# A feed-forward first product by Strassen's scheme over pairs of chunks, in a transformer kernel whose second stage is ordered by timed lines

## The chip, the cores and the metric

The kernel runs on one core of one Trainium2 chip. The metric is the device time of one execution in microseconds; a trace of one profiled execution is there beside it. TensorE (PE in the profile) multiplies matrices, with PEld as its weight load; VectorE is DVE, ScalarE is ACT, GpSimd is POOL, and SyncE (SP) issues nearly all transfers.

## What is computed

Two layers, each an attention block without a softmax over keys and a feed-forward block, on x of 2048 rows (tokens) and 640 columns, all float32:

```python
x = x + A(layernorm(x), wqkv, wo)
x = x + B(layernorm(x), w1, b1, w2, b2)      # and both once more

def A(x, wqkv, wo):                          # 32 heads of 20
    q, k, v = split(x @ wqkv)
    pq, pk = phi(q), phi(k)                  # phi(t) = (t > 0 ? t + 1 : exp(t)) + 1e-6
    kv, z = sum_s(pk[s] v[s]^T), sum_s(pk[s])
    return (pq @ kv / (pq @ z + 1e-6)) @ wo
def B(x, w1, b1, w2, b2):                    # 640 -> 1728 -> 640
    r = max(x @ w1 + b1, 0)
    return (r * r) @ w2 + b2
```

Each float32 operand of a matmul is split into a high and a low part (`split`: ACT copies the value rounded to PE's float32r, DVE subtracts it from the value), and a product is three matmuls: high x low, low x high, high x high (`mm3`, L404 to L408).

## The kernel before, in words

**Tiles and stages.** The 2048 tokens are 16 tiles of 128; four tiles are a group, so there are NG = 4 groups. The 1728 hidden columns are NF = 14 chunks of 128, the last of 64. 640 columns are DC = 5 blocks of 128. In each layer a first stage goes over the 16 tiles (layer norm, q, k and the sums over tokens) and a second stage does the feed-forward over the four groups.

**First stage.** `part` (L494) makes q and k of a tile, `g_part` and `gt_part` the sums over tokens. In layer 0 the `Prep` class (L264) also loads the feed-forward weights, splits them and stores the halves to memory as 24 "units" of 640 KB, two or three a tile by `PREP`. `k_post` (L686) adds k's rows on POOL (L693).

**Second stage, per group and chunk.** `fc1` (L1238) computes a chunk of hidden values for 512 tokens: 5 blocks x 3 matmuls = 15, 512 columns each, in one go into one bank of PSUM; chunk 13 has both halves in one weight tile and takes 10. `act` (L1271) reads the bank: ACT adds b1 and takes the relu (L1276) and the square (L1277), DVE squares again in full (L1280) and makes the low half (L1281); the four instructions follow one another. `fc2` (L1378) multiplies the chunk of the step before with w2: four tiles of 3 matmuls of 512 columns, and a strip of 3 for the last 128 columns of the output, all accumulating in five banks over the 14 chunks. So PE's order is fc1(c), fc2(c-1), fc1(c+1) and so on, each with its long run.

**Side work.** While a group is in the feed-forward, the attention output of the next group's tiles is made beside it: `side` (L1626) puts each step of it at a place (chunk, position after the i-th tile of fc2) from the tables `fast`, `OUTS`, `OUT0` (L38 to L81). Per two tiles it is seven block products of 320 columns (`Pair`, L1500), Strassen's scheme on the product with the 640 x 640 matrix M, whose results go to two banks in turn (`po0`, `po1`); then layer norm, a transpose in blocks of 32 (`blocks_T`, and `blocks_move`, L386, 16 small copies by ACT), the split (`x_split`, L1490) and the addition of b2 to the residual on DVE (`f_bias`, L672, L675). These tables were written by hand; no planner is in the kernel.

**Weights.** Chunks 4 and 7 stay in SBUF (`RESIDENT`); the other units go through a ring of six tiles (`Units`, L298): a used tile is loaded again by `load_ring` (L309, issue L315) from the SP queue. `x1_load`, `x2_store` and the tile loads use the same queue.

**End of a group.** With the last chunk the four accumulated tiles are added to the residual by DVE (`tile_add`, L1372); the strip goes through DVE's transpose and 16 small copies (L1337, L1347, L1365).

Of the kernel before, what the change touches and what calls it, by code (L numbers as in the profile page):

```python
# [13 lines left out]
P = 128  # L14
# [5 lines left out]
NF = 14  # L20
# [8 lines left out]

HR = 6 * DH  # L30
# [5 lines left out]
RESIDENT = (4, 7)  # L36
RING = 6
LATE = ((9, 11, 12, 13, 14, 15), (8, 9, 11, 13, 14, 15))  # L38

PREP = {t: 2 if t > 5 else 3 for t in range(2, 12)}  # L40
# [6 lines left out]
def pair_plan(m0, m1, turn, out, back):  # L47

    return {"blocks0": m0, "blocks1": m1, "turn": turn, "out": out, "back": back}


def fast(b):
    return pair_plan(
        b - 3, b - 2, [(b - 1, 0), (b - 1, 1), (b - 1, 2), (b - 1, 3)],
        {"p1": (b, 0), "p4": (b, 1), "p6": (b, 2), "p7": (b, 3), "p5": (b, 4),
         "p2": (b + 1, 0), "p3": (b + 1, 2)},
        [((b, "post"), (b + 1, 0), (b + 1, 1), (b + 2, 0), (b + 2, 1), (b + 3, 0)),
         ((b + 1, 3), (b + 1, "post"), (b + 2, 0), (b + 2, "post"), (b + 3, "pre"), (b + 3, 4))],
    )

STRIP = ((6, 0), (6, 2), (6, 4), (7, 0), (7, 2))

OUT0 = (fast(4), fast(9))
STAY = 1
FB0 = 0
# [8 lines left out]
LOW_AT = 1  # L76
OUTS = (
    {**fast(2), ("den", 0): ((-4, "post"), (-3, 1)), ("den", 1): ((-3, "post"), (-2, 1)),
     "split1": ((0, "pe"), (0, "post"))},
    fast(9),  # L80
)  # L81

# [6 lines left out]
def kernel(  # L89
# [30 lines left out]
    FB = {"h": 0, "po1": 1, "as": 2, "a0": 3, "a1": 4, "a2": 5, "a3": 6, "po0": 7}  # L120
# [35 lines left out]
    def src_plain(w, r0, c0):  # L156
        return lambda v: [(v, w[r0 : r0 + P, c0 : c0 + D])]

# [9 lines left out]
    def src_w2(c):  # L168
        if c < 13:
            return src_plain(w2, c * P, 0)  # L170
        return lambda v: [(v[:FL], w2[13 * P :, :]), (v[FL:], w2[13 * P :, :])]
# [62 lines left out]
    for g in range(NG):  # L234
        for c in range(NF):
            uses.append((g, "w1", c))
            if c > 0 or g > 0:
                uses.append((g if c else g - 1, "w2", (c - 1) % NF))
    uses.append((NG - 1, "w2", NF - 1))

    def src_unit(nm, c):
        return src_w1(c) if nm == "w1" else src_w2(c)

    def unit_len(nm, c):
        return DC * P if (nm, c) == ("w1", 13) else 2 * D

    def unit_parts(nm, c, u, raw):
        if (nm, c) == ("w1", 13):
            w = u.rearrange("p (d f) -> p d f", d=DC)
            return w[:, :, :FL], w[:, :, FL:], raw[:, : DC * FL].rearrange("p (d f) -> p d f", d=DC)  # L250
        return u[:, :D], u[:, D:], raw

    def split_high(*unit):
        hi, lo, raw = unit_parts(*unit)
        nc.scalar.activation(hi, raw, AF.Copy)

    def split_low(*unit):
        hi, lo, raw = unit_parts(*unit)
        nc.vector.tensor_tensor(out=lo, in0=raw, in1=hi.bitcast(F32), op=ALU.subtract)
# [4 lines left out]
    class Prep:  # L264


        def __init__(self):
            self.todo = [(nm, c) for g, nm, c in uses if g == 0 and c not in RESIDENT]
            self.raws, self.halves, self.done = [], [], []

        def load(self):
            if self.todo:
                nm, c = self.todo.pop(0)
                raw = ftile("st")
                for d, s in src_unit(nm, c)(raw):
                    nc.sync.dma_start(d, s)
                self.raws.append((nm, c, raw))

        def high(self):
            if self.raws:  # L280
                nm, c, raw = self.raws.pop(0)
                u = utile("uprep")[:, : unit_len(nm, c)]
# [3 lines left out]
        def low(self):  # L286
            if self.halves:
                nm, c, u, raw = self.halves.pop(0)
                split_low(nm, c, u, raw)
                self.done.append((nm, c, u))  # L290
# [7 lines left out]
    class Units:  # L298


        def __init__(self):
            self.at = {}
            self.pairs = {}
            self.ring = [u for u in uses if u[2] not in RESIDENT]
            self.stay = [u for u in uses if u[0] == 0 and u[2] in RESIDENT]
            self.free = 0
            self.raws, self.halves = [], []

        def load_ring(self):  # L309

            while self.ring and self.free > 0:
                self.free -= 1
                g, nm, c = self.ring.pop(0)
                u = utile("u")[:, : unit_len(nm, c)]
                nc.sync.dma_start(u.bitcast(F32), kept[nm, c])  # L315
                self.at[g, nm, c] = u

        def place(self):
            _, nm, c = self.stay.pop(0)
            if nm == "w1":  # L320
                self.pairs[c] = wtile("uw")
            i = 2 * D * (nm == "w2")
            self.at[0, nm, c] = u = self.pairs[c][:, i : i + 2 * D]
            return nm, c, u

        def raw_stay(self, dst):

            if len(self.raws) < len(self.stay):
                _, nm, c = self.stay[len(self.raws)]
                for d, s in src_unit(nm, c)(dst):  # L330
                    nc.sync.dma_start(d, s)
                self.raws.append(dst)

        def split_stay(self):
            if self.raws:
# [1428 lines left out]
```

## Time and profile before

| | |
|---|---|
| median of 3 runs | 1334.89 us (1334.78 to 1335.19) |
| span of the profiled execution | 1333.5 us, first to last instruction |
| granted PE clock | 1.000 over the whole span |
| PE / PEld / DVE / ACT / POOL busy | 1328.7 / 1153.0 / 902.6 / 709.0 / 122.8 us |
| second stage, layer 0 and layer 1 | about 249 to 670 us, and 909 us to the end |
| memory traffic | 257.74 MB, 193 GB/s over the span |

The profiled execution's own time is its span and about 1.4 us around it, if it is like the median run. In a row of groups stand the line, engine and operation, the tiles written and read, the shapes and the count; then busy time and the mean of one in ns; then the engine's idle time ahead of them. A matmul's own duration (389 ns for 512 columns) is from its start to its modelled end; matmuls overlap, so their pace is read from start to start. In the table of stretches each engine has its busy time and its count, then come the granted clock, the share of the DMA engines and GB/s.

### The profile page before, as it was taken

To read this page: it belongs to the slowest core of one execution; us is meant where nothing else is said; L and a number is where in the kernel's file an instruction comes from. 1 tells how busy PE (TensorE), PEld (TensorE's weight loads), DVE (VectorE), ACT (ScalarE), POOL (GpSimd) and SP (SyncE) were. 2 spreads that over 40 slices of the span, in tenths; PEclk is the share of its full clock that TensorE was granted. 3 is DMA by queue.
4 is the path that set the end of the run, shared out by engine and by line. 5 is a ranking of instruction groups with operands and counts; after the bars stand their busy time and mean duration, and the time that the engine had idled before them with its cause. 6 is when DMAs were issued, how large, how long until landed. Compare 5 with 4: busy or idle time off the path is not lost.

```text
span 1333.5 us, 18816 instructions
## 1 busy us (share of the span) xinstructions
PE 1328.7 (100%) x6751; PEld 1153.0 (86%) x6751; DVE 902.6 (68%) x1629; ACT 709.0 (53%) x1638; POOL 122.8 (9%) x172
## 2 busy tenths in 40 slices
PE   9999999999999999999999999999999999999998
PEld 8888999988888888888888899998888888888887
DVE  8988888877856766543367678788767567665323
ACT  5888855644544436524547686564534435454131
POOL 1222220000000000000012232100000000000000
PEclk9999999999999999999999999999999999999999
DMA  6788837575656566488521115176547565564654
GB/s 207 260 303 319 273 97 235 195 257 181 220 186 216 153 242 200 150 315 295 194 99 51 49 40 148 40 258 257 177 148 280 149 204 201 194 225 142 245 168 158
DMA packets 101075, 257.74 MB, mean 193 GB/s; under 512 B 12854, under 2 KB 38070, under 8 KB 100310
## 3 DMA queue, kind: packets, MB, share of 16 engines
q1 hardware_dynamic: 99470, 253.85, 56.1%
q10 hardware_dynamic: 1512, 2.69, 0.7%
q8 instruction: 53, 0.87, 0.3%
q14 instruction: 40, 0.33, 0.1%
HBM read 197.80 MB, written 60.13 MB: 193 GB/s over the span
## 4 chain that ended last, share of the span: by engine, by line
PE 100%; ACT 0%; POOL 0%; issue 0%; DVE 0%; POOLq 0%
PE PS L408 38%; PE PS L1321 28%; PE PS L1258 28%; PE PS L429 3%; PE PS L1011 1%; PE PS L1040 1%; PE PS L756 1%; PE PS L557 0%; PE PS L377 0%; PE PS L956 0%; PE PS L773 0%; PE PS L1361 0%; ACT kq L201 0%; ACT xT L777 0%; DVE x L1372 0%
## 5 line engine op out<-in xcount | busy, mean ns | idle before, releaser
L1258 PE MATMUL PS<-xTb,u 128*128 128x512 f32 x1400 | 332.8, 389 | 0.0
L396 ACT ACTIVATE z<-y 32x160 f32<-32x160 f32 x880 | 294.0, 334 | 60.2 <-DVE y L383 50.3
L1258 PEld LDWEIGHTS PS<-xTb,u 128*128 128x128 f32 x1400 | 262.2, 188 | 53.9
L408 PE MATMUL PS<-kq,xT 128*128 128x320 f32 (+2 forms) x1575 | 282.0, 333 | 0.0
L1321 PE MATMUL PS<-u,h 128*128 128x512 f32 (+1 forms) x1125 | 279.7, 389 | 0.0
L408 PEld LDWEIGHTS PS<-kq,xT 128*128 128x128 f32 x1575 | 250.3, 188 | 24.9
L1276 ACT ACTIVATE hr<-PS,b1sb 128x512 f32<-128x512 f32 x104 | 71.5, 687 | 349.2 <-PE PS L1258 347.8
L1321 PEld LDWEIGHTS PS<-u,h 128*128 128x128 f32 x1125 | 208.4, 188 | 39.5
L1280 DVE TENSOR_TENSOR hr<-hr 128x512 f32<-128x512 f32 x104 | 71.3, 685 | 149.5 <-ACT h L1277 149.4
L408 PE MATMUL PS<-kh,xh 128*128 128x512 f32 x480 | 124.3, 392 | 0.0
L367 POOL TENSOR_SCALAR rs<-mv 128x1 f32<-128x1 f32 x62 | 27.9, 450 | 854.7 <-DVE mv L365 854.7
L408 PEld LDWEIGHTS PS<-kh,xh 128*128 128x128 f32 x480 | 87.1, 188 | 14.6
L511 ACT ACTIVATE e<-PS 128x320 f32<-128x320 f32 (+4 forms) x128 | 53.2, 435 | 85.0 <-PE PS L408 77.8
L518 DVE TENSOR_SCALAR e<-e 128x320 f32<-128x320 f32 (+4 forms) x128 | 41.1, 321 | 57.6 <-ACT e L511 57.4
L1321 PE MATMUL PS<-h,u 128*128 128x512 f32 x280 | 79.1, 390 | 0.0
L1281 DVE TENSOR_TENSOR h<-hr,h 128x512 fp32r<-128x512 f32 x104 | 72.0, 693 | 7.8 <-DVE hr L1280 0.5
L693 POOL TENSOR_TENSOR acc<-acc,r 128x640 f32<-128x640 f32 x28 | 50.7, 1811 | 190.0 <-DVE r L519 190.0
L1277 ACT ACTIVATE h<-hr 128x512 fp32r<-128x512 f32 x104 | 65.8, 633 | 3.3
L1321 PEld LDWEIGHTS PS<-h,u 128*128 128x128 f32 x280 | 52.0, 188 | 10.5 <-DVE h L1294 0.4
L1536 DVE TENSOR_TENSOR xr<-PS,xr 128x320 f32<-128x320 f32 x48 | 23.5, 489 | 51.5 <-PE PS L408 50.2
L1258 PE MATMUL PS<-xTb,uw 128*128 128x512 f32 x240 | 57.0, 389 | 0.0
L519 DVE SCALAR_TENSOR_TENSOR r<-PS,e 128x512 f32<-128x512 f32 (+2 forms) x104 | 51.1, 492 | 5.8 <-ACT e L511 2.2
(146 smaller groups left out, 1576.4 us busy)
## 6 DMA issues: line engine op xcount, KB each, us to landing
u<-kept_w SPq DMA_DIRECT2D x184, 640.0 KB, 4.7
x<-x SPq DMA_DIRECT2D x48, 320.0 KB, 5.2
kept_w<-uprep SPq DMA_DIRECT2D x23, 640.0 KB, 5.4
pqt<-pq SPq DMA_DIRECT2D x128, 80.0 KB, 4.5
x<-xr SPq DMA_DIRECT2D x32, 320.0 KB, 2.2
st<-in_B_w_dram SPq DMA_DIRECT2D x22, 320.0 KB, 4.1
pq<-r SPq DMA_DIRECT2D x20, 320.0 KB, 2.3
kept_kq<-kq SPq DMA_DIRECT2D x10, 640.0 KB, 6.8
```

The source lines that it names most:

```text
L396: nc.scalar.activation(d, v, AF.Copy)
L408: nc.tensor.matmul(ps, a, b, start=first and i == 0, stop=last and i == 2)
L511: nc.scalar.activation(self.e[:, a:b], ps, AF.Exp)
L518: nc.vector.tensor_scalar(e, e, 1.0, PHI_EPS, op0=ALU.min, op1=ALU.add)
L519: nc.vector.scalar_tensor_tensor(out=self.r[:, a:b], in0=ps, scalar=0.0, in1=e, op0=ALU.max, op1=ALU.add)
L693: nc.gpsimd.tensor_tensor(out=acc, in0=acc, in1=r, op=ALU.add)
L1258: nc.tensor.matmul(ps, a[:, d, :], bb[:, d, :], start=n == 0, stop=n == len(order) - 1)
L1276: nc.scalar.activation(r, ps, AF.Relu, bias=b1sb[:, c : c + 1])
L1277: nc.scalar.activation(h[:, 0], r, AF.Square)
L1280: nc.vector.tensor_tensor(out=r, in0=r, in1=r, op=ALU.mult)
L1281: nc.vector.tensor_tensor(out=h[:, 1], in0=r, in1=h[:, 0].bitcast(F32), op=ALU.subtract)
L1321: nc.tensor.matmul(ps, l, r, start=(first or new) and k == 0, stop=end and k == len(a) - 1)
```

## The change

**The product.** Chunks 0 to 11 of `fc1` are taken in six pairs. For a pair, the four inner blocks of 640 (two and two, `E`, `F`, `G`, `H` are the weights' combinations) and two halves of 256 tokens make a 2 x 2 product of blocks, done with seven block products where eight were; the fifth block of 128 is done as before (`rest`, 512 columns). The class `Strassen` has five segments: `seg1` (two products, 12 matmuls of 256 columns), `seg2` (one, 6), `seg3` (three, 18), `seg4` (one, 6, and 3 of 512 columns), `seg5` (3 of 512). Partial results are shared by copies between PSUM banks: `copy1` (two by ACT), `copy2` (one by ACT), `add1` and `add2` (DVE). Two banks are used, `h` and `h1`; `h1` takes the place of `po1`, so that the side products have one bank. Tiles stand in the order `POS = (0, 2, 1, 3)` in the group.

```diff
+            def seg1(self):
+                self.product(self.h1[:, :HG], self.w("E", 0), self.x(0, 0), True)
+                self.product(self.h1[:, HG:], self.w("H", 0), self.t("u", 0))
+            def copy1(self):
+                self.s7 = hr_tile("s7")[:, :HG]
+                nc.scalar.activation(self.h0[:, :HG], self.h1[:, :HG], AF.Copy)
+                nc.scalar.activation(self.s7, self.h1[:, HG:], AF.Copy)
+            def seg2(self):
+                self.product(self.h1[:, :HG], self.w("G", 0), self.t("u", 1))
+            def copy2(self):
+                nc.scalar.activation(self.h0[:, HG:], self.h1[:, :HG], AF.Copy)
+            def add1(self):
+                l = self.h1[:, :HG]
+                nc.vector.tensor_tensor(out=l, in0=l, in1=self.s7, op=ALU.add)
+            def seg3(self):
+                self.product(self.h0[:, :HG], self.w("E", 1), self.x(1, 0))
+                self.product(self.h0[:, HG:], self.w("H", 1), self.t("v", 0))
+                self.product(self.h1[:, :HG], self.w("F", 0), self.t("v", 1))
+            def add2(self):
+                nc.vector.tensor_tensor(out=self.h1[:, HG:], in0=self.h0[:, HG:], in1=self.s7, op=ALU.add)
+            def seg4(self):
+                self.product(self.h0[:, HG:], self.w("G", 1), self.x(1, 1))
+                self.rest(self.h0, 1)
+            def seg5(self):
+                self.rest(self.h1, 0)
```

**What it needs beside it.** The weights' combinations are made in the first stage of layer 0 by four sums per pair on POOL, and stored as units of 512 KB; `w2` of chunks 8 to 11 is split only in the second stage. The tokens' combinations are four sums per two tiles, on DVE or POOL (`t_sums`), and splits of them (`t_split`). The addition of b2 goes from DVE to POOL.

```diff
+        def sums(self, c):
+            r0, r1 = self.pair[c]
+            ...
+                nc.gpsimd.tensor_tensor(out=out, in0=x, in1=y, op=op)
...
+        def t_sums(t, eng):
+            ...
+                eng[0].tensor_tensor(out=out, in0=x, in1=y, op=ALU.subtract)
...
         def f_bias(t):
             v = xr.pop(t)
-            nc.vector.tensor_tensor(out=v, in0=v, in1=b2bc, op=ALU.add)
+            nc.gpsimd.tensor_tensor(out=v, in0=v, in1=b2bc, op=ALU.add)
+            yield
             nc.sync.dma_start(x1d[t], v)
...
-RESIDENT = (4, 7)
 RING = 6
+STEPS = (("p", 13), ("p", 12), *(("w", i) for i in range(NW)))
+FIRST, LAST = 13, 11
+POS = (0, 2, 1, 3)
...
-PREP = {t: 2 if t > 5 else 3 for t in range(2, 12)}
+AFTER = 8
+PREP = {t: 4 if t in (3, 5, 7) else 3 for t in range(2, 13)}
```

No chunk is resident any more; the ring has seven tiles, and a group reads 40 units in the order of their use.

**The order.** The hand-written tables go. A planner, the class `Clock`, keeps a time for each engine and for the transfers, with costs in the code (for instance 0.14 us and 0.95 ns a column on ACT, 0.08 us and 1.04 ns on DVE, 0.2 us and 2.4 ns on POOL, n x (columns/2400 + 0.0133) us on PE). The work is a list of "lines", generators that yield an engine, a cost and the function that issues the instructions, or a need (`need`, `until`, a free buffer). `run` always issues PE's next step from the line that can go on first (by rank where equal), after `fill` has issued all work of the other engines that ends by then. So the order is fixed when the program is built. `fc1_line` is:

```diff
+                    yield "PE", pe_cost(12, HG), st.seg1
+                    yield "until", lambda: slots["hr"]
+                    yield "ready", ck.chain(
+                        "ACT", 2 * cost("ACT", HG), st.copy1, max(main.ready, free[0], take("hr"))
+                    )
+                    yield "PE", pe_cost(6, HG), st.seg2
+                    at = main.ready
+                    yield "ready", ck.chain("ACT", cost("ACT", HG), st.copy2, at)
+                    yield "ready", ck.chain("DVE", cost("DVE", HG), st.add1, at)
+                    yield "PE", pe_cost(18, HG), st.seg3
+                    yield "ready", ck.chain("DVE", cost("DVE", HG), st.add2, main.ready)
+                    yield "PE", pe_cost(6, HG) + pe_cost(3, GT), st.seg4
+                    turned(g, 2 * c, st.h0, 0)
+                    yield "PE", pe_cost(3, GT), st.seg5
+                    turned(g, 2 * c + 1, st.h1, 1)
```

`fc2_line` yields one step per tile (3 matmuls), `pair_line` one per block product, and `x_line`, `t_line`, `q_line`, `strip_line`, `ring_line`, `next_line` the rest; a block move can go to ACT or DVE, a square or a sum to DVE or POOL, whichever the planner has free first.

1052 lines of the change are left out of this document (713 added, 339 removed).

## The prediction

> **What bounds the kernel now.** I read the first page, then PE's waits, the chain of work, the groups by form, and a few stretches in order of time.
>
> ```profile
> span 1333.5 us, 18816 instructions
> PE 1328.7 (100%) x6751; PEld 1153.0 (86%) x6751; DVE 902.6 (68%) x1629; ACT 709.0 (53%) x1638; POOL 122.8 (9%) x172
> PE 100%; ACT 0%; POOL 0%; issue 0%; DVE 0%; POOLq 0%
> ```
> ```profile
> PE PS L557 <- POOL ident masks.py:199: 1.4, 1, 1.4
> ```
>
> TensorE is busy from end to end, the chain that ends last is PE alone, and in PE's list of waits there is one entry, 1.4 us before the first transpose. So every matmul taken away shows in full, and every wait that is added shows in full too. A "busy PE" could still hide slow matmuls, so their real pace comes next, from starts:
>
> ```profile
> 699.73 0.85 PE L408 MATMUL PS<-kh,xh 128*128 128x512 f32 x3
> 700.42 1.95 PE L408 MATMUL PS<-kq,xT 128*128 128x256 f32 x15
> 702.21 0.86 PE L408 MATMUL PS<-kh,xh 128*128 128x512 f32 x3
> ```
> ```profile
> 1320.51 5.67 PE PS L1321 x25
> ```
> ```profile
> L1258 PE MATMUL PS<-xTb,u 128*128 128x512 f32 x1400 | 332.8, 389 | 0.0
> L408 PE MATMUL PS<-kq,xT 128*128 128x256 f32 x285 | 37.1, 282 | 0.0
> L1258 PE MATMUL PS<-xTb,uw 128*128 128x512 f32 x240 | 57.0, 389 | 0.0
> ```
>
> Twenty-five matmuls of 512 columns took 5.67 us: 0.2268 each. Fifteen of 256 columns took 702.21 - 700.42 = 1.79 us from first start to next start: 0.119 each, each with weights of its own. I use 0.120. The busy time of that group gives 37.1/285 = 0.130; it counts the last one's tail beside the next matmul, so it is the upper bound.
>
> **The change, part by part.**
>
> *Products.* The first product now has 1400 + 240 = 1640 matmuls of 512 columns (205 in each of 8 groups of tokens). Behind the change a group has six pairs of chunks, each with 42 matmuls of 256 and 6 of 512, beside chunks 12 and 13 as before (25 of 512): 252 and 61, so 2016 and 488 in all. Gone: 1152 x 0.2268 = 261.3. New: 2016 x 0.120 = 241.9. Net **-19.4 us**; with 0.119 it is -21.4, with 0.130 +0.8. The second product and the seven-product pairs of the attention output keep their matmuls.
>
> [...] The sum goes by the rows.
>
> *New waits.* Before, a chunk was one unbroken run of 15 matmuls into one bank. Now a pair is five segments (12, 6, 18, 9 and 3 matmuls), and between them ACT copies quarters of PSUM (three copies of 256 columns) and DVE adds (two). PE's next segment waits for these; what is queued behind the waiting matmul on PE is everything else, so it must be covered by matmuls put between. Prices:
>
> ```profile
> 600.14 3.56 PE L1258 MATMUL PS<-xTb,uw 128*128 128x512 f32 x15
> 603.54 2.88 PE L1321 MATMUL PS<-u,h 128*128 128x512 f32 x12
> 603.74 0.69 ACT L1276 ACTIVATE hr<-PS,b1sb 128x512 f32<-128x512 f32 x1 [5.45 <-PE PS L1258]
> ```
> ```profile
> L511 ACT ACTIVATE e<-PS 128x256 f32<-128x256 f32 x19 | 7.3, 385 | 0.4
> L1468 DVE TENSOR_TENSOR z<-z 128x256 f32<-128x256 f32 x48 | 20.4, 424 | 1.5
> L1372 DVE TENSOR_TENSOR x<-PS,x 128x512 f32<-128x512 f32 x32 | 20.9, 685 | 27.8 <-PE PS L1321 20.0 <-DMA x<-x 7.8
> L1498 DVE TENSOR_TENSOR xTb<-z,xTb 128x640 fp32r<-128x640 f32 x24 | 19.7, 822 | 29.5 <-ACT xTb L1496 29.5
> L675 DVE TENSOR_TENSOR xr<-xr,b2bc 128x640 f32<-128x640 f32 x32 | 26.0, 814 | 0.0
> L693 POOL TENSOR_TENSOR acc<-acc,r 128x640 f32<-128x640 f32 x28 | 50.7, 1811 | 190.0 <-DVE r L519 190.0
> ```
>
> From the next matmul's start to ACT's start: 603.74 - 603.54 = 0.20 us. With an estimate of 0.05 back to PE, two copies cost 0.20 + 2 x 0.385 + 0.05 = 1.02, one copy 0.64, one addition 0.67. In the order in which the changed program issues PE's instructions, most gaps hold six matmuls of the second product (1.36 us), so they are covered with 0.34 and 0.7 to spare. Uncovered are: the first pair of each layer, where nothing stands in the first two gaps (1.02 + 0.64, twice: **3.3 us**); and the step from the first group to the second in layer 0, where DVE is to split the last tile of the second group only behind the four additions of the first group's output, and PE has nothing left (0.20 + 0.685 + 0.82 + 0.05 = **1.75 us**). Lower bound for the other gaps is nothing; the upper bound stands with the rivals.
>
> *VectorE and ScalarE.* Both have room: DVE is busy 68%. Per layer the change adds 48 additions, 32 or so sums and 16 splits to DVE and takes 16 biases off it (0.814 each); ACT gets 72 copies and 16 splits and loses about a tenth of its block moves. Taken off an engine that PE does not wait for, this gains nothing.
>
> *POOL.* The 32 additions of b2 go to POOL, as do 24 sums of weights in the first stage and some 28 short sums beside the feed-forward. This is where the profile warns. In order of time:
>
> ```profile
> 53.67 1.63 POOL L693 TENSOR_TENSOR acc<-acc,r 128x640 f32<-128x640 f32 x1 [7.13 <-DVE r L519]
> ```
> ```profile
> 53.89 0.56 DVE L519 SCALAR_TENSOR_TENSOR r<-PS,e 128x384 f32<-128x384 f32 x1
> 54.37 1.61 DVE L147 TENSOR_TENSOR xh<-xt,xh 128x640 fp32r<-128x640 f32 x1
> ```
> ```profile
> L147 DVE TENSOR_TENSOR xT<-z,xT x29: 815/817/826, 38.1 to 832.8; 128x640 fp32r<-128x640 f32 x29
> ```
>
> The same subtraction takes 0.817 where POOL rests and 1.61 where POOL adds two SBUF tiles: 0.79 us late, and it ends 0.68 us after POOL does, as if it had waited. [...] A single hit of 0.79 is nearly covered (0.7 to spare), a double one is not: I take 0.25 each, 2.5 us. In each layer the first four biases run in a row just behind the first pair, DVE loses 4 x 0.79 = 3.2 us there, and I take half for PE: 3 us. Together **5.5 us**, bounds 0 and 32 x 1.63 = 52.
>
> *First stage of layer 0.* 36 units of weights are made instead of 24, but smaller:
>
> ```profile
> 42.00:54.00 12.00, 12.00 (x59) 9.99 (x59) 11.33 (x23) 10.67 (x27) 2.01 (x3) 1.00 0.87 301
> ...
> sum 120.00, PE 120.00 PEld 104.35 DVE 103.17 ACT 102.14 POOL 27.36; mean PE 12.00 PEld 10.43 DVE 10.32 ACT 10.21 POOL 2.74
> ```
>
> Over 30 to 150 us DVE is busy 103 of 120. New: some 7 us of splits, and waits for 24 sums on POOL of 0.65 each (an estimate, 1.63 x 256/640), 15.6 at most. With half of that 118 of 120: still covered, so 0; with all of it 125, so 5 is the other bound.
>
> *Transfers.* No weights stay resident: per group 24 units of 512 KB, 15 of 640 and one of 320 are read, not 23 of 640 and one of 320, 7.3 MB more per 107 us, 68 GB/s. A busy stretch shows what that means:
>
> ```profile
> u<-kept_w SPq DMA_DIRECT2D x184, 640.0 KB, 4.7
> ```
> ```profile
> 460.00:550.00 90.00, 90.00 (x431) 76.73 (x430) 56.12 (x98) 37.27 (x83) 2.38 (x6) 1.00 0.60 205
> 550.00:650.00 100.00, 100.00 (x447) 83.13 (x447) 40.77 (x67) 46.04 (x111) 3.96 (x11) 1.00 0.74 269
> ```
> ```profile
> DMA to landing us min/median/max: 3.7/4.6/8.3
> ```
>
> The last line is that of the 25 loads in 550 to 650, at 269 GB/s, the rate that the other groups (205) will come to. The tightest load (H's unit) is released 7.6 us of matmuls ahead of its use: covered at the median, 1 us short at the slowest. I take 1 us with all other small waits.
>
> *Sum.* Span 1333.5 - 19.4 + 3.3 + 1.75 + 5.5 + 1 = 1325.7. The median of the runs, 1334.89, lies 1.4 above the span; with that **1327 us**, 0.6% faster.
>
> **The rivals.**
>
> *All covered.* PE's filler absorbs the POOL hits too, since a PE that has waited gives the others time: 1334.9 - 19.4 + 3.3 and little else, 1317 to 1320. For it: the typical gap has 0.34 to 0.7 us to spare. Against: before had no wait at all to begin with, and the order is fixed when the program is built.
>
> *POOL's lock, slower than before.* Each of the 32 biases makes DVE late, a late addition stalls PE, and PE's stall is not made good, since the list was drawn up without this. If each costs PE 1 us (1.63 less 0.6 to spare) the sum is 1327 - 5.5 + 32 = 1354. It decides from (19.4 - 5.1 - 1)/32 = 0.42 us per bias. For it: the 1.61 row. [...]
>
> *Weights late.* If H's unit lands like the slowest of that stretch every time, 48 x 1 us: 1327 + 48 = 1375; it decides from 0.16 us per pair. Against: medians of 4.6 and smaller units.
>
> *The products do not get cheaper.* At 0.130 per matmul of 256 the gain is gone: 1327 + 20.2 = 1347. Against: the 1.79 us for fifteen.
>
> **How the numbers follow.** Forecast 0.53 (own range 1320 to 1334), all covered 0.12, lock 0.18, weights late 0.13, no cheaper 0.04. A measurement of this kernel tells 0.2% (2.7 us: 1332.2 to 1337.6) from no change. Faster: 0.12 + 0.48 = 0.60. Same: the upper edge of the forecast 0.05, 0.04 of the lock, 0.02 of weights = 0.11. Slower: 0.14 + 0.11 + 0.04 = 0.29. The range 1317 to 1346 leaves out what lies below all covered (0.03), the worse half of the lock (0.07), half of weights late (0.06) and the last rival (0.04).
>
> **What would show it.** PE's waits, empty now, should sum to about 11 us, with the first pair's two gaps in each layer (about 1.0 and 0.6) and one of about 1.7 at the first group's end; matmuls of 256 columns start 0.120 apart; DVE subtractions beside POOL's biases take 1.6 rather than 0.8. I am wrong if PE's waits behind DVE or behind loads pass 13 us, or if 256 columns take 0.130.

## The result and the profile after

The changed kernel takes **1388.15 us** (1384.60 to 1392.37, 4 runs), the one before 1335.04 us beside it: a ratio of 1.0398 (95% interval 1.0376 to 1.0420), 4% slower. The forecast was 1327.

The first page of the changed kernel:

```profile
span 1388.4 us, 21426 instructions
PE 1337.4 (96%) x7616; PEld 1184.3 (85%) x7616; DVE 1014.8 (73%) x1883; ACT 744.8 (54%) x1724; POOL 235.1 (17%) x264
PE 55%; DVE 19%; DMA 13%; ACT 5%; issue 3%; SPq 3%; POOL 1%; ACTq 0%; DVEq 0%; POOLq 0%
```

PE is "busy" for only 9 us more than before, yet the span grew by 54.9. The chain of work tells more: it was PE alone, and now 45% of it lies elsewhere. PE's list of waits had one entry, 1.4 us, and now has seventeen, 47.4 us in all. The four largest, and the four behind transfers (us in total, times, longest; the other nine left out):

```profile
PE PS L567 <- DVE xr L1813: 7.9, 6, 2.8
PE PS L1646 <- DVE h L1592: 6.5, 3, 3.5
PE PS L567 <- DVE r L679: 4.9, 3, 2.3
PE PS L1497 <- DVE PS L1539: 4.4, 5, 1.1
PE PS L1497 <- DMA u<-kept_wH: 3.7, 3, 1.8
PE PS L1646 <- DMA u<-kept_w: 2.4, 3, 1.1
PE PS L1497 <- DMA u<-kept_wG: 1.3, 1, 1.3
PE PS L1497 <- DMA u<-kept_wE: 0.6, 1, 0.6
```

Of the 47.4 us, 30.7 end with a DVE instruction, though DVE is busy only 73%. So the next question is what DVE itself waited for. `pqt` is a tile of pq (phi(q) of the first stage), loaded back from memory for the attention output of the next group. Of DVE's list, the line that counts, in the changed kernel:

```profile
DVE pr L777 <- DMA pqt<-pq: 20.4, 11, 4.1
```

and all that DVE waited for transfers in the kernel before, where pqt isn't among it:

```profile
DVE x L1372 <- DMA x<-x: 7.8, 2, 3.9
DVE bn L363 <- DMA xt<-in_A_x_dram: 2.5, 1, 2.5
DVE uu L1536 <- DMA u<-kept_w: 1.1, 1, 1.1
```

Such a wait of DVE is not idle room: what PE needs from DVE next stands in DVE's order behind the instruction that waits (the rows of a late tile, below, show it). The stretches of the changed kernel, cut at the first matmul of the first product (L1463) and the last of the second (L1646) in each layer, the last one up to the end of the span (the columns are as before: length, busy time of PE, PEld, DVE, ACT and POOL with counts, granted clock, DMA share, GB/s):

```profile
0.00:261.80 261.80, 253.40 (x1431) 226.98 (x1431) 225.62 (x430) 185.77 (x433) 77.02 (x91) 0.98 0.69 232
261.80:706.40 444.60, 422.85 (x2396) 371.84 (x2397) 308.69 (x562) 210.71 (x482) 50.71 (x60) 0.98 0.79 272
...
946.90:1388.40 441.50, 421.27 (x2406) 368.66 (x2406) 296.43 (x535) 193.10 (x432) 54.09 (x57) 1.00 0.75 256
```

| stage, us | before | forecast | after | over the forecast |
|---|---|---|---|---|
| first, layer 0 | 249.0 | 249.0 | 261.8 | 12.8 |
| second, layer 0 | 420.4 | 417.3 | 444.6 | 27.3 |
| first, layer 1 | 239.8 | 239.8 | 240.5 | 0.7 |
| second, layer 1 | 424.4 | 419.6 | 441.5 | 21.9 |

(The forecast's stages are those of before with its terms put where they belong: 9.7 off each second stage, the waits on.) The first stage of layer 0, the two second stages, and a granted clock below 1 are to be explained. Three places show how the time goes.

**A late tile of pqt.** In order of time, SP, DVE and PE:

```profile
512.86 2.10 SPq L766 DMA_DIRECT2D pqt<-pq  x4
518.71 0.85 PE L1646 MATMUL PS<-u,h 128*128 128x512 f32 x3
521.07 0.82 DVE L777 TENSOR_TENSOR pr<-pqt,zbc 128x640 f32<-128x640 f32 x1 [4.09 <-DMA pqt<-pq]
521.81 0.48 DVE L1813 TENSOR_TENSOR xr<-PS,xr 128x320 f32<-128x320 f32 x1
522.35 1.97 PE L567 MATMUL PS<-uT,uS 128*128 128x320 f32 x6 [2.80 <-DVE xr L1813]
```

SP needs 2.1 us to issue a tile's four loads, and DVE can use the tile 6 us later. The planner put `q_line`'s first instruction (L777) on DVE by its own landing time, which was too early. DVE stands 4.09 us in front of it; behind it is the addition (L1813) that frees the one bank of the side products, and PE stands 2.80 us for that.

**The first pair of a layer and the four biases.** PE, DVE and POOL:

```profile
269.58 0.87 PE L1497 MATMUL PS<-tx,u 128*128 128x256 f32 x6
271.25 0.98 PE L1497 MATMUL PS<-tx,u 128*128 128x256 f32 x6 [0.80 <-ACT s L1519]
272.75 0.98 PE L1497 MATMUL PS<-xTb,u 128*128 128x256 f32 x6 [0.52 <-ACT PS L1525]
272.79 7.18 POOL L835 TENSOR_TENSOR xr<-xr,b2bc 128x640 f32<-128x640 f32 x4
273.07 1.57 DVE L1591 CAST h<-hr 64x512 fp32r<-64x512 f32 x1
274.68 1.92 DVE L1592 TENSOR_TENSOR h<-hr,h 64x512 fp32r<-64x512 f32 x1
276.65 1.19 PE L1646 MATMUL PS<-u,h 128*128 128x512 f32 x4 [1.49 <-DVE h L1592]
393.87 0.41 DVE L1591 CAST h<-hr 64x512 fp32r<-64x512 f32 x1
394.32 0.69 DVE L1592 TENSOR_TENSOR h<-hr,h 64x512 fp32r<-64x512 f32 x1
```

The two gaps of a first pair are as forecast: 271.25 - 269.58 - 6 x 0.12 = 0.95, and 0.78, against 1.02 and 0.64. Beside POOL's four biases, DVE's cast takes 1.57 instead of 0.41 and the subtraction 1.92 instead of 0.69 (last two rows, without POOL).

**The first stage of layer 0.** POOL, SP and PE:

```profile
152.11 4.33 POOL L450 TENSOR_TENSOR st<-st 128x256 f32<-128x256 f32 x4 [4.66 <-DMA pq<-r]
153.56 1.17 SPq L355 DMA_DIRECT2D kept_kq<-kq  x1
168.20 0.32 SPq L407 DMA_DIRECT2D kept_wH<-uprep  x1
171.15 3.71 SPq L766 DMA_DIRECT2D pqt<-pq  x4
196.57 3.41 PE L567 MATMUL PS<-kq,xT 128*128 128x320 f32 x15 [2.19 <-DVE r L679]
```

Four sums of a pair of weights take 4.33 us on POOL, not 4 x 0.65. The units made from them come a token tile later, SP stands from 154.7 to 168.2 in front of the store of one, and the loads behind it, which the end of the stage needs, are late.

### The profile page after: what moved, and what is told of

It reads as the page before. It is cut to its first block, busy times and chain, and to the rows that moved or that the text cites. A ratio compares the mean times of both kernels' runs of the same rounds, so it can differ in the third digit from the quotient of the medians.

```text
span 1388.4 us, 21426 instructions
## 1 busy us (share of the span) xinstructions
PE 1337.4 (96%) x7616; PEld 1184.3 (85%) x7616; DVE 1014.8 (73%) x1883; ACT 744.8 (54%) x1724; POOL 235.1 (17%) x264
## 4 chain that ended last, share of the span: by engine, by line
PE 55%; DVE 19%; DMA 13%; ACT 5%; issue 3%; SPq 3%; POOL 1%; ACTq 0%; DVEq 0%; POOLq 0%
PE PS L567 21%; PE PS L1646 17%; PE PS L1497 12%; DMA pqt<-pq 5%; PE PS L1507 3%; ACT z L555 2%; DMA u<-kept_w 2%; SPq L766 1%; DMA u<-kept_wH 1%; PE PS L1463 1%; DVE e L678 1%; DMA u<-kept_wF 1%; DVE bn L517 1%; DVE z L553 1%; DVE uprep L404 1%
## 5 line engine op out<-in xcount | busy, mean ns | idle before, releaser
L1646 PE MATMUL PS<-u,h 128*128 128x512 f32 x1318 | 342.0, 395 | 8.9 <-DVE h L1592 6.5
L555 ACT ACTIVATE z<-y 32x160 f32<-32x160 f32 x781 | 261.1, 334 | 57.8 <-DVE y L542 37.6
L1646 PEld LDWEIGHTS PS<-u,h 128*128 128x128 f32 x1318 | 242.6, 191 | 55.6 <-DVE h L1592 7.3
L1497 PE MATMUL PS<-tx,u 128*128 128x256 f32 x1152 | 162.7, 284 | 8.5 <-DMA u<-kept_wH 3.7
L1497 PEld LDWEIGHTS PS<-tx,u 128*128 128x128 f32 x1152 | 150.7, 192 | 15.2 <-ACT s L1519 5.2
L1497 PEld LDWEIGHTS PS<-xTb,u 128*128 128x128 f32 x864 | 120.9, 192 | 24.6 <-DVE PS L1539 6.8
L1497 PE MATMUL PS<-xTb,u 128*128 128x256 f32 x864 | 129.4, 286 | 9.8 <-DVE PS L1539 4.4
L1646 PE MATMUL PS<-h,u 128*128 128x512 f32 x328 | 92.6, 391 | 0.0
L678 DVE TENSOR_SCALAR e<-e 128x320 f32<-128x320 f32 (+4 forms) x128 | 49.7, 388 | 47.6 <-ACT e L670 46.9
L1507 PE MATMUL PS<-xTb,u 128*128 128x512 f32 x288 | 76.8, 393 | 0.0
L1646 PEld LDWEIGHTS PS<-h,u 128*128 128x128 f32 x328 | 59.9, 188 | 11.0
```

The source lines that it names most:

```text
L555: nc.scalar.activation(d, v, AF.Copy)
L678: nc.vector.tensor_scalar(e, e, 1.0, PHI_EPS, op0=ALU.min, op1=ALU.add)
L1497: nc.tensor.matmul(ps, l[:, d], r[:, d], start=start and d == 0 and n == 0, stop=d == 1 and n == 2, skip_group_check=True,)
L1507: nc.tensor.matmul(ps, l[:, k], r, start=False, stop=n == 2, skip_group_check=True)
L1646: nc.tensor.matmul(ps, l, r, start=(first or new) and k == 0, stop=end and k == len(a) - 1)
```

## The experiments

"Before" of the same chip lay between 1335.01 and 1335.24 (medians) beside all of these runs. The changed kernel's own runs spread over 8 us, so that differences below about 4 us between two versions say little; then the stages of the trace are compared. Medians in us, 95% intervals of the ratio to the kernel before, and the four stages of each profiled execution:

| run | median | ratio | first 0 | second 0 | first 1 | second 1 |
|---|---|---|---|---|---|---|
| after | 1388.15 | 1.0376 to 1.0420 | 261.8 | 444.6 | 240.5 | 441.5 |
| e1_bias_dve | 1400.91 | 1.0481 to 1.0538 | 261.6 | 449.9 | 240.6 | 443.4 |
| e3_all_dve | 1386.90 | 1.0377 to 1.0413 | 264.2 | 437.9 | 240.2 | 443.4 |
| e4_old_bias_pool | 1342.17 | 1.0038 to 1.0068 | 250.8 | 422.2 | 241.3 | 426.2 |
| e5_late_plan | 1386.98 | 1.0377 to 1.0408 | 261.5 | 443.2 | 240.6 | 438.7 |
| e6_no_segment_work | 1382.16 | 1.0333 to 1.0364 | 262.1 | 441.9 | 240.5 | 436.4 |
| e7_both | 1369.67 | 1.0245 to 1.0279 | 262.6 | 434.3 | 240.2 | 430.0 |
| e8_loads_first | 1384.26 | 1.0352 to 1.0384 | 256.2 | 442.8 | 240.5 | 440.3 |
| e9_bias_pieces | 1379.77 | 1.0324 to 1.0363 | 260.2 | 441.3 | 240.6 | 436.0 |
| e10_pieces_late_first | 1370.72 | 1.0249 to 1.0279 | 254.9 | 437.2 | 240.6 | 433.9 |
| e11_half_loads_dve | 1366.57 | 1.0220 to 1.0251 | 263.8 | 429.6 | 240.2 | 431.7 |
| e12_half_loads | 1351.95 | 1.0109 to 1.0143 | 251.0 | 428.5 | 240.6 | 430.6 |
| e13_three_dve | 1366.70 | 1.0209 to 1.0245 | 255.1 | 433.9 | 240.1 | 430.8 |
| e14_old_more_traffic | 1335.15 | 0.9991 to 1.0010 | 249.1 | 420.4 | 239.8 | 424.4 |
| e15_half_no_segments | 1349.94 | 1.0095 to 1.0125 | 251.5 | 425.2 | 240.6 | 429.7 |
| e16_half_no_bias | 1337.18 | 1.0003 to 1.0022 | 250.8 | 421.7 | 240.6 | 421.5 |
| e17_pqt_one_load | 1369.24 | 1.0227 to 1.0269 | 257.1 | 433.7 | 240.6 | 436.9 |
| e18_regrouped_store | 1367.55 | 1.0215 to 1.0251 | 256.2 | 437.5 | 241.2 | 431.1 |
| e19_pqt_four_rows | 1384.04 | 1.0343 to 1.0386 | 260.6 | 442.7 | 240.5 | 439.1 |

Three theories stood at the start. A: POOL's work lengthens DVE's instructions (1.92 instead of 0.69 above; the recorded texts call it the lock, and that there is one was not shown). B: loads land (their data is in place) later than the plan counts on. C: the gaps between segments aren't covered.

Not all edits are equally clean, since the planner draws up a new order when a cost or an engine changes. In e8, e9, e12, e16, e17 and e19 the instructions of PE, DVE and ACT stand in the order of the changed kernel, so these runs show the price of what was edited alone. In e1, e3, e5, e6, e7, e10, e11, e13, e15 and e18 PE's order departs from it after about 1500 of its 7616 matmuls, so another order is part of what they measure.

### One cause at a time (e1, e3, e4, e5)

```diff
 e1, f_bias                       (and its cost in bias(): "POOL" -> "DVE")
-            nc.gpsimd.tensor_tensor(out=v, in0=v, in1=b2bc, op=ALU.add)
+            nc.vector.tensor_tensor(out=v, in0=v, in1=b2bc, op=ALU.add)
 e3: e1, and
-            eng = {"DVE": nc.vector, "POOL": nc.gpsimd}
+            eng = {"DVE": nc.vector}
-        list(t_sums(0, [nc.gpsimd]))
+        list(t_sums(0, [nc.vector]))
-                nc.gpsimd.tensor_tensor(out=out, in0=x, in1=y, op=op)     # Prep.sums
+                nc.vector.tensor_tensor(out=out, in0=x, in1=y, op=op)
 e4: the kernel before, f_bias
-            nc.vector.tensor_tensor(out=v, in0=v, in1=b2bc, op=ALU.add)
+            nc.gpsimd.tensor_tensor(out=v, in0=v, in1=b2bc, op=ALU.add)
 e5: Clock.go
-                self.t["DMA"] = max(self.t["DMA"], start + 1.3) + each / 0.39
-                line.got = self.got = self.t["DMA"] + 0.7 + HOP
+                self.t["DMA"] = max(self.t["DMA"], start + 1.3) + each / 0.33
+                line.got = self.got = self.t["DMA"] + 2.4 + HOP
```

> The changed kernel with its 32 biases (f_bias) on DVE instead of POOL, planner price included. Theory A (POOL's lock: the biases lengthen DVE by some 25 us in the two second stages, and PE waits for that): PE's waits behind DVE at the start of each second stage (274 to 279 us, 3 us a layer) go, about 1365 us in all. Theory B (loads land later than the planner counts on, and hold up PE directly or through the head of DVE's queue): those few us only, 1380 to 1386, since waits for pqt and weights stay. Theory C (the gaps between segments are not covered, whoever does the biases): 1388, or slower, as DVE gets 26 us of work more.

> All that the change put on POOL goes to DVE: biases, the short sums of inputs, the squares that the planner may give to POOL, and the 24 sums of weights in the first stage. Theory A: second stages 30 us shorter together, the first stage of layer 0 back from 262 to about 254: 1350 us. Theory B: first stage unchanged at about 262 (its longest waits stand behind loads of the output weights), second stages 5 us shorter: 1383. Theory C: no gain, 1388 or above.

> The kernel before with one word changed: its 32 biases on POOL. It has no segments and no new transfers, so it shows the lock by itself. Theory A: 32 x 0.4 to 1.0 us, 1348 to 1367 us. Theory B or C: DVE is late but PE has work in store, under 3 us: 1335 to 1338.

> Only the planner's model of transfers is changed: 0.33 instead of 0.39 bytes per ps and 2.4 instead of 0.7 us behind the last one, so that it takes loads to land about 2 us later, as the trace shows. Theory B: DVE's instructions that need pqt and PE's that need weights are put later in their queues, the waits for them (about 24 us by the trace) mostly go: 1365 to 1372 us. Theory A or C: nothing, 1384 to 1392.

Neither A nor B came out. e1 was 12.8 us slower than the change, e3 and e5 the same as it within their spread. Only e4 gave a price: 7.2 us for the 32 biases on POOL in the kernel before, 0.22 each, below what A expected and above what B and C did. One line of PE's waits tells what happened in e1, and then in e5:

```profile
PE PS L1463 <- DVE xTb L1777: 16.6, 2, 10.4
```
```profile
PE PS L1497 <- DVE PS L1539: 14.9, 7, 4.5
```

In e1 the waits beside the first four biases are gone (those behind h at L1592 fall from 6.5 to 1.5). But at the end of the first group DVE comes to the last tile's layer norm (L532) only at 376.1 us, at 368.0 in the changed kernel, and PE stands 10.4 us for that tile's split. Six biases, 0.8 us or more each, stand on DVE ahead of that layer norm; DVE's order is another one, too, and it waits 28.6 us in all for pqt (20.4 in the changed kernel), so the share of the biases isn't shown. In e5 DVE waits 1.0 us for pqt in all and PE 2.3 for weights; but five instructions that were put later (L678 to L793, 3.4 us) now stand on DVE ahead of an addition between segments (L1539), beside the four biases, and PE stands 4.5 us for it, once in each layer. Each edit took away its wait, and others filled the place.

### Both, and the segments (e6, e7)

```diff
 e6: copy1, copy2, add1, add2 do nothing, fc1_line doesn't wait for them; in seg3
-                self.product(self.h0[:, :HG], self.w("E", 1), self.x(1, 0))
+                self.product(self.h0[:, :HG], self.w("E", 1), self.x(1, 0), True)
-                self.product(self.h0[:, HG:], self.w("H", 1), self.t("v", 0))
+                self.product(self.h0[:, HG:], self.w("H", 1), self.t("v", 0), True)
 e7: e3 and e5 together
```

> The changed kernel without the work between the segments of a pair: the three copies of 256 columns on ACT and the two additions on DVE are left out (so the quarters aren't combined, and the first product isn't the reference's), with all matmuls, loads, biases and splits kept; nothing stands between one segment and the next. If the gaps between segments are what PE pays for (C), 30 us or more go: 1355. If what is late is the rest, that is DVE under POOL's lock and the loads (A and B), the waits move to the next place and few us go: 1375 to 1385.

> All of POOL's new work on DVE together with the later landing times in the plan, each of which by itself left 1385 to 1387 because the other wait took over. If lock and late loads are two separate causes that cover each other: 1365 to 1372 us, with PE's waits behind loads and behind lengthened DVE instructions both gone. If the bound is DVE's own work, or the plan's waits simply replace the others: 1380 to 1390.

Together the two edits that gave 1.2 us each give 18.5 (e7). That fits A and B as separate causes that cover for each other; as e3, e5 and e7 each run another order, the covering is argued from them and not shown. That both causes exist is shown below, without a change of order (e12 and e17 for the loads, e16 for the biases). Leaving out all that stands between the segments (e6) gives only 6.0, so C is a small part of what PE pays for.

### The first stage, and shorter biases (e8, e9)

```diff
 e8: at each tile of the first stage
+            if t >= 13:
+                b_load_pq(t - 13)
+                load_vo(2 * t - 26)
+                load_vo(2 * t - 25)
             if layer == 0:
                 prep.store()
                 if 10 <= t < 10 + DC:
                     keep_kq(t - 10, 0)
...
-            if t >= 13:
-                b_load_pq(t - 13)
-                load_vo(2 * t - 26)
-                load_vo(2 * t - 25)
 e9: f_bias
-            nc.gpsimd.tensor_tensor(out=v, in0=v, in1=b2bc, op=ALU.add)
+            for s in (slice(P * c, P * c + P) for c in range(DC)):
+                nc.gpsimd.tensor_tensor(out=v[:, s], in0=v[:, s], in1=b2bc[:, s], op=ALU.add)
```

> Only the order on SP in the first stage of layer 0 is changed: at each step the loads of pqt and of the weights of the output are issued ahead of the stores of prepared weights. In the trace SP stands from 154.7 to 168.2 us behind the store of an H unit that DVE has not made, 13.5 us; in the kernel before it did not. If that is why PE waits at 194 and 199 us, the first stage gets 4 to 6 us shorter (256 to 258 us from 261.8), and all 1379 to 1384. If DVE's load or POOL's sums are the cause: 261 to 262, and 1384 to 1392.

> Each bias on POOL in five instructions of 128 columns instead of one of 640; the plan and DVE's work stay. If a DVE instruction waits until POOL's instruction ends (A), the hits get short (0.3 us rather than up to 1.3) and the waits at 274 to 279 and 431 to 447 us shrink: 1370 to 1378 us. If the lock isn't held by the instruction, or if it costs little beside the loads: 1384 to 1392.

e8 is as expected in its stage: 256.2 instead of 261.8, 5.6 us. e9 gives 8.4 us, less than A hoped for, with the late loads still there.

### Traffic, and two joined versions (e10 to e13)

```diff
 e11: e3, and only half of each unit is loaded (one unit whole); the products read it in place of the low half too
-            nc.sync.dma_start(u.bitcast(F32), kept[key[1:]])
+            n = slice(0, u.shape[1] // (1 if key[1:] == ("w1", 13) else 2)); nc.sync.dma_start(u[:, n].bitcast(F32), kept[key[1:]][:, n])
 e12: the same half loads in the changed kernel; e8; and in Prep.sums
-                nc.gpsimd.tensor_tensor(out=out, in0=x, in1=y, op=op)
+                pass
 e10: e9 + e5 + e8
 e13: e8, the second stages of e3, and e5 with 0.36 and 1.6
```

> Three edits that have each run alone (or nearly so) put together: biases on POOL in five pieces (1379.8 alone), later landing times in the plan (1387.0 alone), loads ahead of stores in the first stage (1384.3 alone). If the lock and the late loads hide each other, as the pair of all-DVE and later landing showed (1369.7), the sum is larger than the 14 us that the three make singly: 1360 to 1368 us, with the first stage at about 255. If they only add: 1372 to 1376.

> As e3 (nothing of the new work on POOL), but each load of a weight unit from memory fetches only its high half, and the products read that half in place of the low one too (the result is that of other weights; all matmuls and their sizes stay). The traffic of the second stages falls by nearly half and the plan is unchanged. If late loads are what remains without the lock: 1355 to 1365 us, second stages of about 425 each, pqt's landing near 3.5 us. If DVE's own work bounds it, now 8 us a layer more than before: 1380 to 1387.

> Two edits in stages that don't overlap. Second stages: half loads as in e11, with POOL's work left as the change has it. If loads are late by bandwidth, each second stage loses 8 to 12 us (435 and 430); if the lock alone carries the loss, they stay at 443 and 440. First stage of layer 0: loads ahead of stores as in e8 (256.2), and the 24 sums of weights left out (the units G, H, F are then of other weights). If the sums are the rest of its loss: 250 to 252; if the loss is in the larger number of splits and transfers: 255 to 256.

> The other way to join the edits: second-stage work on DVE, sums of weights left on POOL, loads first, and a plan with a milder correction (0.36 and 1.6 us). With the milder correction PE's planned waits are shorter but loads may be late again. Same causes, so about 1362 us if the correction suffices, 1370 to 1376 if waits behind loads come back.

e12 is the run that tells most. Its second stages, and DVE's wait for pqt in it:

```profile
251.00:679.50 428.50, 417.55 (x2395) 368.37 (x2396) 308.48 (x562) 210.62 (x482) 50.67 (x60) 1.00 0.57 182
920.10:1350.70 430.60, 417.61 (x2406) 367.69 (x2406) 297.88 (x535) 193.16 (x432) 54.63 (x57) 1.00 0.52 161
```
```profile
DVE pr L777 <- DMA pqt<-pq: 3.7, 3, 1.9
```

In these stages DVE, ACT and POOL do the same work in the same order, and with the same busy time, as in the changed kernel, and SP issues the same transfers in the same order; only the loads are on time (pqt is there 3.6 us after its issue, median, instead of 5.8). The second stages are 16.1 and 10.9 us shorter and the granted clock is back at 1.00. So **27 us of the loss are late loads**, more of it by way of DVE than directly: in the two second stages PE's waits behind units fall from 8.0 us to 1.6, those behind DVE from 24.5 to 12.5, and PE spends 3.4 us at half clock where it spent 17.1 (below), which is worth up to 6.8 more. Its first stage: 251.0, another 5.2 us for the sums of weights beyond e8. e11 has the same second stages without anything on POOL, 2 us apart in sum: with loads on time it made no difference whether DVE did the additions (more work) or POOL (longer DVE instructions), as far as e11's other order lets one say. e10 and e13 only add up; they end where e7 did.

### What is left, and why the loads are late (e14 to e17, e19)

```diff
 e14: the kernel before, load_ring: behind each load of a unit
+                ("x", nm, c) in kept or keep(("x", nm, c), [P, u.shape[1] // 2]); nc.sync.dma_start(kept["x", nm, c], kept[nm, c][:, : u.shape[1] // 2])
 e15: e12 + e6
 e16: e12, and in f_bias
-            nc.gpsimd.tensor_tensor(out=v, in0=v, in1=b2bc, op=ALU.add)
 e17: the changed kernel, b_load_pq: four loads of 80 KB that regroup the tile become
+                nc.sync.dma_start(pq[t], pqd[t])
 e19: the same bytes as e17, in four loads
+                    nc.sync.dma_start(
+                        pq[t][j * B32 : (j + 1) * B32], pqd[t][j * B32 : (j + 1) * B32]
+                    )
```

> The kernel before, with a copy of half a unit (320 KB) from memory to memory behind each load of a weight unit in the second stages: 7.4 MB more per group, as much as the change adds, with one more instruction on SP each. Its first product needs a unit only every 25 matmuls and nothing on DVE or ACT answers to PE inside a chunk. If the traffic as such makes loads late, this costs like the change's loads did, 10 to 25 us: 1345 to 1360. If it is the short lead that the seven products and the plan leave, the old order covers it: 1335 to 1339.

> As e12, with the work between the segments left out too (three copies, two additions a pair). With late loads the segments' work was worth 6 us (e6). With loads on time it shows its own price: if the gaps between segments are what is left of the two second stages (428.5 and 430.6, about 34 us above the forecast's products), these fall to about 415 to 420 each and all to 1330; if lock and the start of the stage are what is left, they fall by 3 to 5 us each, 1343 to 1346.

> As e12, with the 32 biases left out altogether (b2 isn't added), so that neither POOL's lock nor DVE pays for them; POOL keeps only a few short sums. If the lock is the larger part of what is left with loads on time: 12 us or more less, 1340. If it is the segments and the start of the stages: 3 to 6 us less, 1346 to 1349.

> The changed kernel with each tile of pqt fetched by one instruction of 320 KB as it lies in memory, instead of four of 80 KB that regroup it (so the numbers in it stand in other places): the same bytes, a quarter of the instructions on SP and larger packets. If loads are late by the number of issues and packets: 10 us or more less, 1375 to 1379. If by bytes: 1385 to 1390.

> As e17, but in four instructions of 80 KB (32 rows as they lie in memory): the number of issues of the change, with e17's packets of whole rows. If the number of issues on SP makes loads late: as the change, 1383 to 1390. If the size of the packets does: as e17, 1366 to 1371.

- **More traffic costs the kernel before nothing.** With 7.5 MB more read per group, and as much written, it takes 1335.15 against 1335.17 (e14). The units land in 5.3 us instead of 4.7 (medians), and its order leaves them that time. But pqt isn't later there (4.3 against 4.5), and nothing of the extra traffic ends in SBUF, so how the old order would stand a late pqt isn't shown.
- **The number of issues decides for pqt.** One load a tile instead of four, with the tile's numbers left in other places, takes 18.9 us off (e17); four loads of whole rows take off 4 (e19), inside the spread of the changed kernel. SP is free earlier, and pqt is complete 6.3 us after its only issue, where four issues of 2.1 us come ahead of a 5.8 (medians). The planner counts 0.08 us of SP for an issue (`start += 0.08` in `Clock.go`); those of pqt took 0.30 to 1.45 us, 0.43 at the median. DVE's waits for pqt, in e17 and in e19:

```profile
DVE pr L773 <- DMA pqt<-pq: 7.8, 4, 3.4
```
```profile
DVE pr L776 <- DMA pqt<-pq: 16.8, 10, 4.1
```

- **The biases cost 15.9 us with loads on time** (e16: 421.7 and 421.5 against 428.5 and 430.6, in the same order), the segments' work 4.2 (e15, in another order: 425.2 and 429.7; 2.0 by the medians).

With half loads, no sums and no biases, e16 takes 1337.18, 0.03 to 0.22% above the kernel before. What PE still waits for in it, apart from the first transpose:

```profile
PE PS L1496 <- DVE hr L1603: 2.0, 2, 1.0
PE PS L1645 <- DVE h L1591: 2.0, 1, 2.0
PE PS L1496 <- ACT s L1518: 1.6, 2, 0.8
```

With a 1.5 behind the last split they are the first pair of each layer and the step to the second group. In all other pairs the gaps are covered in this run but for one of 0.4, as forecast.

### A version from the findings (e18)

```diff
 e18: e8 + e9, and pq is regrouped when it is stored, so that each tile is one load
+        def store_pq(t, r):
+            v = pqd[t].rearrange("(j q) (i r) -> i q j r", i=JB, j=JB)
+            for i in range(JB):
+                nc.sync.dma_start(v[i], r[i * B32 : (i + 1) * B32].rearrange("q (j r) -> q j r", j=JB))
```

> The best correct version that the runs point to, three edits: pq is regrouped when it is stored (four instructions of 80 KB a tile, mostly in the first stage) so that each tile of pqt is one load of 320 KB as in e17 (1369.2); loads ahead of stores in the first stage (e8, -4); biases on POOL in five pieces (e9, -8). If they add: 1354 to 1360, first stage at 251 to 256, second stages at 430 each. It does not reach the kernel before unless the waits for lock and loads hid more than these runs show; if the extra stores make the first stage late on SP: 1360 to 1366.

1367.55: the three edits don't add up (e17 alone gave 1369.24). PE's longest list entry in it is now the H units (5.7 us in four waits), and DVE waits 16.2 us for pqt where it waited 7.8 in e17: the plan is a new one, and loads are late in other places.

The four joined versions that leave nothing out (e7, e10, e13, e18) lie between 1366.7 and 1370.7, all at least 2% above the kernel before. None beats it.

## Why the prediction was wrong, step by step

The step that failed is **Transfers** ("I take 1 us with all other small waits"): 27 us in its place. It compared the landing time (from the issue until the data is in place) with the lead (from the issue to the use) for the weights that PE itself waits for. PE's direct waits behind units are 8.0 us (3.7, 2.4, 1.3 and 0.6). What it left out is that transfers also stand at the head of DVE's queue, and that a load waits its turn on SP behind the others. The rows for it were there: pqt is loaded by the same queue, and its median landing of 4.5 us stood on the page of the kernel before. The change's plan places DVE's use of pqt by a landing time of its own, too early with that traffic (about 2 us later in the plan, and DVE's waits for pqt fell to 1.0, e5); the old tables placed it without a wait.

- *Products.* Right. The 19.4 us stand, since 256 columns stay 0.119 to 0.120 apart (443.68, 444.39, 445.11 for the starts of groups of six):

```profile
443.68 0.88 PE L1497 MATMUL PS<-xTb,u 128*128 128x256 f32 x6
444.39 0.88 PE L1497 MATMUL PS<-tx,u 128*128 128x256 f32 x6
445.11 1.55 PE L1646 MATMUL PS<-u,h 128*128 128x512 f32 x6
```

- *New waits.* Right where a time was given. The 0.05 back to PE was an estimate without a row; in the changed kernel PE starts 0.05 us after DVE's subtraction (276.60 to 276.65, above) and 0.06 after its addition (522.29 to 522.35). A first pair has 0.95 and 0.78; the step to the second group is 385.58 - 381.18 - 12 x 0.2268 = 1.68 against 1.75:

```profile
381.18 2.88 PE L1646 MATMUL PS<-u,h 128*128 128x512 f32 x12
385.58 5.96 PE L1463 MATMUL PS<-xTb,u 128*128 128x512 f32 x25 [1.52 <-DVE xTb L1777]
395.06 1.99 PE L1646 MATMUL PS<-u,h 128*128 128x512 f32 x5 [3.52 <-DVE h L1592]
```

  Left out was what comes before and after: chunk 13's bank, which DVE drains late (the `hr` waits, 1.0 a layer), the split ahead of chunk 13 (0.6), and the wait in the last row, 3.52. With loads on time and no biases that one is 2.0, and the second stages are still 12.8 us above the forecast's other terms; these waits are 5.3 of it (2.0, 1.3 and 2.0), 3.4 us at half clock behind the last of them (from 371.9 us) up to 1.7, and I did not follow the rest.
- *VectorE and ScalarE.* "Both have room" was true as a sum and useless as an argument. DVE's busy time in a second stage is 308.7 us with the loss and 308.5 without it (e12). What counts is the order in its queue.
- *POOL.* 15.9 us in place of 5.5, mis-sized by a factor of three, inside the bounds of 0 and 52. No run shows the 2.5 us in the 5.5, 0.25 for each addition behind a bias; measured are the 15.9 for all 32, 0.50 each (e16). I had counted too few of DVE's instructions: a cast and a copy were lengthened as well, 1.57 instead of 0.41 and 1.51 instead of 0.25 (below). That POOL is to blame, rather than the additions themselves, is not shown: on DVE they cost as much (e11, e1). A price of 0.82 for an addition on DVE is off PE's path only where DVE isn't what PE stands behind.
- *First stage of layer 0.* 12.8 in place of 0, bound 5. I had counted DVE's work. Shown are 5.6 for SP's order (e8) and 5.2 for the sums (e12), each in the order of the changed kernel; the sums put on DVE instead (e3) made it 264.2. The last 2.0 stay open. I had not asked when the units end: `PREP` now runs one tile longer, and the last stores stand in front of the loads on SP.
- *The rivals.* "Weights late" (1375) came nearest in time and in kind, by another road. "POOL's lock" (1354) is a part of the truth, 15.9 us. The line "I am wrong if PE's waits behind DVE or behind loads pass 13 us" was the right alarm: those behind DVE are 30.7.
- *The clock* was in no step; it is worth about 11 us, which are part of the terms above and below, not a term beside them.

The sum over the forecast, 62.7: loads 26 and biases 10.4 more than forecast, first stage 12.8, first stage of layer 1 0.7, starts of the stages and small gaps 12.8. These are read from edits one on top of the other; in another order they would share out differently, as e7 against e3 and e5 suggests.

## What to carry to other kernels

When PE waits behind an engine that is far from busy, look at what that engine waits for at the head of its queue, transfers first; this matmul-bound kernel paid for late loads that DVE's queue stood behind (27 us with those that PE itself waited for, e12). If an edit that removes a cause changes nothing, remove it together with the next one before dropping it: here two edits worth 1.2 us each were worth 18.5 together. Prefer an edit that leaves the order of every engine as it is: with a planner, another order comes with most edits and is measured with them. On a queue shared by loads and stores (SP here) look at the issues and at their order: four issues a tile instead of one, for the same bytes of pqt, made 14.8 us (1384.04 in e19, 1369.24 in e17), and a store that waited 13.5 us for its data held up the loads behind it (5.6 us of the first stage, e8).

## What the runs showed of the hardware

**Half clock after short gaps.** The granted clock, 0.999 to 1.000 in all runs of the kernel before, was 0.988 to 0.995 in those of the changed one. The loss isn't spread out: in the profiled execution there are eight steps of 3.4 us at half clock (two of them in a row), each behind one or two gaps of PE; three lie in the first stage of layer 0, five in the second stages. One of them, the step ahead of it, and a step with a gap that left the clock alone, by the table of stretches (PE's busy time comes second, the clock third from the end):

```profile
976.00:979.40 3.40, 3.40 (x9) 2.65 (x8) 1.90 (x4) 1.15 (x2) 0.00 (x0) 0.50 1.03 414
972.60:976.00 3.40, 1.76 (x9) 1.45 (x10) 3.30 (x7) 1.28 (x3) 0.00 (x0) 1.00 1.01 374
1061.30:1064.70 3.40, 1.99 (x9) 1.31 (x7) 1.64 (x3) 0.53 (x1) 1.47 (x1) 1.00 1.04 321
```

At half clock matmuls of 512 columns start 0.427 us apart instead of 0.227. Over the eight steps the matmuls' starts lie about 11 us behind their full pace. So a stall of about 2 us ahead of such a step cost up to 1.7 more, half of 3.4. One such step came behind a gap of 2.29 us that began at 160.6, another behind gaps of 1.70 and 0.61 with matmuls between, at 972 to 975; behind a gap of 2.20 us that began at 1063.3 the clock stayed at 1.00. What tells them apart in this trace is PE's idle time within one step, when the trace is cut into steps of 3.413 us (the length of a half-clock step in its clock records) that start and end with the half-clock ones. The seven steps right ahead of a half-clock stretch held 1.6 us of idle time or more (3.40 - 1.76 at 972.6), and no other, from 6.6 us on, held more than 1.52; the gap at 1063 lies across the border of two steps and left 3.40 - 1.99 = 1.4 in the first of them. It is one trace, and that the idle time within a step is the cause was not shown.

**What POOL lengthens.** Beside POOL's biases a cast and a copy with one SBUF input took longer too: the cast 1.57 us instead of 0.41 (L1591, above), and a copy of 32 x 160 took 1.51 us beside two biases, 0.25 without:

```profile
442.45 3.54 POOL L835 TENSOR_TENSOR xr<-xr,b2bc 128x640 f32<-128x640 f32 x2
443.07 1.51 DVE L553 COPY z<-y 32x160 f32<-32x160 f32 x1
447.37 0.25 DVE L553 COPY z<-y 32x160 f32<-32x160 f32 x1
```
